# Pooling attention and an MLP mixer in one kernel: rows 0 to 4 of the plan laid out anew, and the end of the fast units reordered

## The chip, the cores and the metric

The kernel runs on one core of one Trainium2 chip. The metric is the time of one execution on the device, in microseconds (us). The profile's names for the engines are PE (matmuls), DVE (vector), ACT (scalar), POOL (GpSimd) and SP (whose queue issues DMAs). POOL's queue issues DMAs too, and an instruction that waits there holds up the loads behind it.

## What is computed

Attention over keys and values that are averaged over 8 neighbouring rows (576 rows become 72), and then an MLP mixer: token mixing with a residual, channel mixing with a residual.

```python
# q, k, v: (8, 8, 576, 64) float32
k_p = k.reshape(B, H, Sp, pool, D).mean(axis=3)          # pool = 8, Sp = 72
v_p = v.reshape(B, H, Sp, pool, D).mean(axis=3)
scores = scale * np.matmul(q, k_p.transpose(0, 1, 3, 2))
scores = scores - np.max(scores, axis=-1, keepdims=True)
attn = np.exp(scores)
attn = attn / (np.sum(attn, axis=-1, keepdims=True) + 1e-09)
x = np.matmul(attn, v_p)                                 # then (8, 576, 512)
h = np.maximum(x.transpose(0, 2, 1) @ w_tok1, 0.0) @ w_tok2   # 576 -> 256 -> 576
u = x + h.transpose(0, 2, 1)
h2 = np.maximum(u @ w_ch1, 0.0) @ w_ch2                  # 512 -> 1536 -> 512
out = u + h2                                             # (8, 576, 512) float32
```

## The kernel before

All matmuls are bf16. The program has a head, in which batch 0 is brought through attention and token mixing, and then nine units. Unit n (0 to 7) does the channel mixing of the first 512 rows of batch n; unit 8 does that of the last 64 rows of all batches together (u_tails). A unit has 45 steps, 0 to 44, each a few matmuls. Between the steps of a unit the work of the batches ahead is issued, by hand: PLAN has a row for each unit, which names for a step what is issued behind it. Each engine runs its own instructions in the order in which they were issued, and engines wait for each other by semaphores, so PLAN is the order of every engine's queue. A name such as 2.K0 is batch 2's operation K0; the Tile framework's manual schedule keeps the order as written.

**The units.** Steps 0 to 23 are the first product (l1_tile): 12 blocks of four matmuls of 512 columns, two steps each (L526), and an ACT relu into GT (L530). Steps 24 to 44 are the second product as seven products of 12 matmuls of 256 columns, three steps each (L680), in the manner of Strassen and Winograd: sums of parts of GT (=1 to =4, one DVE operation of 128x1536 each, L554 and L566, in g_sums) are multiplied by sums of parts of w_ch2 (w0 to w3, L554, made once in unit 0). Each product's bank is evacuated by a DVE addition (L723) into s1, s2, s4, s5 or the output tile o, which SP stores (L545). Units 7 and 8 use a scheme with seven products for the first layer too (l1_fast, L641): 21 products of four matmuls in the order of ORDER, named A to C for three groups and 1 to 7 for the product; some are kept on ACT, others added by DVE (L625) and then put through a relu (L628 on DVE, L654 on ACT).

**Attention of one batch b.** lq, lk, lv: loads, on POOL's queue (L121, L131). K0, K1, V0, V1: the sums over 8 rows for four heads, three POOL operations (L177, L178, then L181 for keys or L183 for values); k0, v0, v1 are the same on DVE; vpool0 and vpool1 do it with matmuls on PE. kpT: the keys transposed on PE (L225) and copied by ACT (L227). Q0, Q1: the queries transposed in blocks on DVE (L287). s0 to s2: scores on PE (L300), exp on ACT (L309). av0 to av4: 128 rows each (av4: the last 64), eight matmuls (L388) into one of two PSUM buffers (ps_two, "p" in the profile, shared with the scores), then on DVE a reciprocal of the denominators (L392) and one multiplication (L331). aw0 to aw4: the same with the multiplication as eight ACT instructions of 64 columns.

**Token mixing.** at0, at1: five matmuls (L400) and an ACT relu (L402). u0 to u4: two matmuls (L422; u4 for two batches together, L417) and a DVE addition of the residual (L423). Then u has to be transposed for the channel mixing. For batches 0 to 2, t0 to t3: PE transposes (L431), copied by ACT (L432). Batches 3 to 7 go by way of DRAM: M0, M2, M4 write u out (L441, on SP), M reads back the parts of M0 and M2 in four DMAs (L453, SP, tile v) and MT that of M4, and T0 to T5 are DVE block transposes of v (L465).

**Gates.** "g" is a memset of one element on DVE (L809) and a copy of it on POOL (L810). POOL's queue, the loads in it among it, goes no further than that copy before DVE has come to the memset; the next memset waits for the copy before it.

**PSUM.** Beside the two buffers of ps_two there are four banks, p1a to p1d, which take and give hand out in the order in which they come free, when the program is recorded.

Of the kernel before, what the change touches and what calls it, by code (L numbers as in the profile page):

```python
# [35 lines left out]
def kernel(  # L36
# [565 lines left out]
    def l1_fast(n, uT):  # L602
# [20 lines left out]
        def add(g, k, ps, row, half):  # L623
            dst = GT[:, half, row * NH + 2 * g:row * NH + 2 * g + 2]
            nc.vector.tensor_tensor(out=dst, in0=ps, in1=kept[g, k], op=ALU.add)  # L625
            if g > 0:
# [1 line left out]
                nc.vector.tensor_scalar(out=dst, in0=dst, scalar1=0.0, scalar2=None, op0=ALU.max)  # L628
# [32 lines left out]
    ORDER = "A1 A2 B1 B2 A6 C1 C2 A5 A7 B6 A3 B5 B7 A4 C6 B3 C5 C7 B4 C3 C4"  # L661

    def unit_fast(n, u):
        last = n == B
# [63 lines left out]
        def store_part(cols, engines):  # L728
            def go(i):
                if len(engines) == 2:  # L730
                    engines[i].dma_start(out=tail_rows(1, cols)[:, i], in_=ob[:, i, cols])
                elif i == 1:
                    engines[0].dma_start(out=tail_rows(1, cols), in_=ob[:, :, cols])
# [4 lines left out]
        x, y = bank(last), bank()  # L738
        s1 = keep("s1")
        yield from product(x, lambda m: GT[:, 0, m], lambda m: w_ch2[:, m, lo], True,  # L740
                           plus(part(s1), part(x), residual(0, 0)), last)
# [142 lines left out]
```

## Time and profile before

| | us |
|---|---|
| median of 3 runs | 264.68 (263.78 to 265.58) |
| the profiled execution | 265.02 |
| its span, first to last instruction | 263.2 |

The granted clock of PE was 0.999 in it. The units stand in the trace like this (by the first matmul of line 526 in each, from PE's timeline): unit 0 from 24.32 us, 1 from 57.40, 2 from 87.46, 3 from 115.53, 4 from 146.26, 5 from 170.54. A row of a timeline gives the start in us, the duration, engine and line, the operation, out and in by the program's names, partitions by elements, the count of like instructions run together, and in brackets the engine's idle time before it with what ended it.

```profile
core 0: us, PE busy (x) PEld busy (x) DVE busy (x) ACT busy (x) POOL busy (x), PEclk, DMA share, GB/s
24.32:57.40 33.08, 31.78 (x271) 20.20 (x274) 25.59 (x46) 15.89 (x26) 18.60 (x22) 1.00 1.22 208
57.40:87.46 30.06, 29.49 (x287) 18.29 (x293) 21.66 (x37) 19.49 (x32) 28.93 (x26) 1.00 0.54 100
87.46:115.53 28.07, 27.70 (x241) 16.55 (x241) 21.01 (x42) 13.06 (x21) 25.38 (x30) 1.00 0.69 144
115.53:146.26 30.73, 29.66 (x255) 17.81 (x255) 24.97 (x51) 13.55 (x23) 26.28 (x23) 1.00 0.75 156
146.26:170.54 24.28, 24.23 (x197) 14.79 (x197) 17.84 (x35) 11.98 (x20) 16.94 (x18) 1.00 0.53 126
```

These are units 0 to 4: length, busy time of each engine with its instructions, the granted clock, the DMA share and rate.

### The profile page before, as it was taken

The page shows a single profiled execution, that of the slowest core. Times are in us where ns is not written, and L with a number is a line of the kernel's source. Part 1 is how long each engine was busy: PE and PEld are TensorE (multiplying, and loading weights), DVE is VectorE, ACT ScalarE, POOL GpSimd, SP SyncE. Part 2 cuts the span into 40 slices and gives each one's busy share as a digit, 9 for nine tenths or more (in the row PEclk, how much of TensorE's full clock was granted, in tenths as well). Part 3 has the DMA queues.
Part 4 walks back from the last instruction along what each step waited for, and adds up shares of the span by engine and source line. Part 5 has one row for each costly group of instructions (what it writes and reads, how often), then busy time and mean ns, then how long its engine had stood idle before and what let it go on. Part 6 is the DMA issues. An engine that isn't in the chain of part 4 may idle for free. (4 is left out here: it accounts for less than half of the span.)

```text
span 263.2 us, 5488 instructions
## 1 busy us (share of the span) xinstructions
PE 254.0 (97%) x2171; PEld 167.7 (64%) x2193; DVE 195.7 (74%) x400; ACT 119.0 (45%) x195; POOL 166.1 (63%) x177
## 2 busy tenths in 40 slices
PE   8999999989999999999998999999999999999994
PEld 2785466754667544774476447754684478888883
DVE  3557469986787665896599686863696389999994
ACT  2355763149537466415640565255625421712700
POOL 8667326899999999978879992798407922100000
PEclk9999999999999999999999999999999999999999
DMA  7999999993079928599645932650315052602404
GB/s 148 187 198 207 205 207 208 206 225 75 4 127 145 163 86 168 133 185 249 127 152 94 215 130 66 97 156 1 126 37 161 2 157 63 181 0 49 114 2 159
DMA packets 31706, 34.31 MB, mean 130 GB/s; under 512 B 3136, under 2 KB 23744, under 8 KB 31680
## 3 DMA queue, kind: packets, MB, share of 16 engines
q0 software_dynamic: 17632, 17.64, 42.4%
q1 hardware_dynamic: 13632, 15.93, 20.4%
q8 instruction: 17, 0.28, 0.5%
q10 hardware_dynamic: 416, 0.39, 0.5%
q14 instruction: 9, 0.07, 0.1%
HBM read 38.99 MB, written 12.58 MB: 196 GB/s over the span
## 5 line engine op out<-in xcount | busy, mean ns | idle before, releaser
L526 PEld LDWEIGHTS <-w_ch 128*128 128x128 bf16 x336 | 30.2, 98 | 33.4 <-issue 2.7
L680 PEld LDWEIGHTS <-area 128*128 128x128 bf16 x432 | 41.4, 98 | 7.5 <-issue 1.0
L810 POOL COPY flag<-flag 1x1 f32<-1x1 f32 x41 | 12.5, 304 | 43.1 <-DVE flag L809 43.0
L309 ACT ACTIVATE ex<-p 72x768 bf16<-72x768 f32 x42 | 31.5, 802 | 17.1 <-PE p L300 17.1
L680 PEld LDWEIGHTS <-GT 128*128 128x128 bf16 x324 | 30.7, 98 | 7.5 <-issue 1.6
L178 POOL TENSOR_TENSOR t<-t 72x512 f32<-72x512 f32 x23 | 32.4, 1409 | 1.8
L526 PE MATMUL p1c<-uT,w_ch 128*128 128x512 bf16 x100 | 28.0, 379 | 0.2
L177 POOL TENSOR_TENSOR t<-kr 72x1024 f32<-72x1024 bf16 x12 | 25.5, 2121 | 0.4
L177 POOL TENSOR_TENSOR t<-vr 72x1024 f32<-72x1024 bf16 x11 | 23.4, 2123 | 2.4 <-DMA vr<-in_v_dram 1.9
L331 DVE TENSOR_TENSOR x<-p,den 128x512 bf16<-128x512 f32 x32 | 22.1, 691 | 1.1
L526 PE MATMUL p1b<-uT,w_ch 128*128 128x512 bf16 x75 | 21.3, 379 | 0.4 <-issue 0.2
L530 ACT ACTIVATE GT<-p1c 128x512 bf16<-128x512 f32 x26 | 15.5, 597 | 12.3 <-PE p1c L526 8.5
L526 PE MATMUL p1a<-uT,w_ch 128*128 128x512 bf16 x72 | 20.5, 379 | 0.3
L526 PE MATMUL p1d<-uT,w_ch 128*128 128x512 bf16 x74 | 19.9, 379 | 0.2 <-issue 0.2
L530 ACT ACTIVATE GT<-p1b 128x512 bf16<-128x512 f32 x20 | 11.9, 596 | 15.3 <-PE p1b L526 8.8
L530 ACT ACTIVATE GT<-p1d 128x512 bf16<-128x512 f32 x19 | 11.4, 599 | 14.0 <-PE p1d L526 8.5
L388 PEld LDWEIGHTS <-ex 72*128 72x128 bf16 x280 | 12.9, 98 | 7.5 <-DVE x L331 2.0
L423 DVE TENSOR_TENSOR u<-p1d,x 128x512 bf16<-128x512 f32 x11 | 8.0, 727 | 11.9 <-PE p1d L422 11.0
L554 DVE TENSOR_TENSOR area<-GT 128x1536 bf16<-128x1536 bf16 x9 | 11.4, 1263 | 6.9 <-ACT AT L402 5.2
L388 PE MATMUL p<-vp,ex 72*128 72x65 bf16 x280 | 14.4, 194 | 1.0 <-DVE x L331 0.5
L121 POOL DMA_DIRECT2D kr<-in_k_dram x17 | 10.9, 646 | 5.4 <-PE p1c L526 2.0
L680 PE MATMUL p1a<-area,area 128*128 128x256 bf16 x108 | 14.3, 273 | 0.0
(235 smaller groups left out, 536.6 us busy)
## 6 DMA issues: line engine op xcount, KB each, us to landing
out_dram<-o SPq DMA_DIRECT2D x32, 256.0 KB, 4.1
qb<-in_q_dram POOLq DMA_DIRECT2D x7, 576.0 KB, 10.3
kr<-in_k_dram POOLq DMA_DIRECT2D x7, 512.0 KB, 8.9
vr<-in_v_dram POOLq DMA_DIRECT2D x7, 512.0 KB, 14.4
w_ch<-in_moe_w_ch_dram POOLq DMA_DIRECT2D x5, 512.0 KB, 14.5
mem<-u SPq DMA_DIRECT2D x10, 256.0 KB, 2.2
v<-mem SPq DMA_DIRECT2D x20, 128.0 KB, 2.9
area<-in_q_dram SPq DMA_DIRECT2D x2, 288.0 KB, 3.0
```

The costliest lines, as they stand in the source:

```text
L121: nc.gpsimd.dma_start(out=t[j0:j1, h0:h1].rearrange("j h i d -> j h (i d)"), in_=src[b, h0:h1].rearrange("h (j i) d -> j h (i d)", i=POOL) ...
L177: eng.tensor_tensor(out=t4[:, 0:n], in0=t[:, hs, 0:4], in1=t[:, hs, 4:8], op=ALU.add)
L178: eng.tensor_tensor(out=t4[:, 0:n, 0:2], in0=t4[:, 0:n, 0:2], in1=t4[:, 0:n, 2:4], op=ALU.add)
L309: nc.scalar.activation(out=dst, in_=src, func=AF.Exp, scale=scale)
L331: nc.vector.tensor_tensor(out=dst, in0=view, in1=den[:, :, :, None].broadcast_to([n, a, 4, D]), op=ALU.mult)
L388: nc.tensor.matmul(out=ps[:, h // 4, (h % 4) * (D + 1):(h % 4 + 1) * (D + 1)], lhsT=st["ex"][:, h * S + n0:h * S + n0 + P], rhs=st["vp"][: ...
L423: nc.vector.tensor_tensor(out=rows_of(c), in0=blocked(ps), in1=blocked(x), op=ALU.add)
L526: nc.tensor.matmul(out=ps, lhsT=w_ch1[:, kk, m * P:(m + 1) * P], rhs=uT[kk], start=(kk == 0), stop=(kk == 3))
L530: nc.scalar.activation(out=GT[:, :, m, :], in_=ps.rearrange("p (h n) -> p h n", h=2), func=AF.Relu)
L554: eng.tensor_tensor(out=out, in0=a, in1=b, op=ALU.subtract)
L680: nc.tensor.matmul(out=ps[i] if split else ps[:, i], lhsT=chunk(u, i, a(m)), rhs=w(m), start=start and m == 0 and (i == 0 or split), stop= ...
L810: nc.gpsimd.tensor_copy(out=flag[:, 1:2], in_=flag[:, 0:1])
```

## The change

HEAD and rows 5 to 8 of PLAN stay. Rows 0 to 4 are written anew: the same operations at other steps, with these differences in kind: 1.av0, 2.av3, 4.av1 and 4.av2 become 1.aw0, 2.aw3, 4.aw1 and 4.aw2 (normalised on ACT); 5.K0 on POOL becomes 5.k0 on DVE; 36 gates instead of 41 in these and the later rows together, at other steps, with the loads of batches 5 to 7 behind other ones; the block transfers of batches 3 to 5 (M, MT, T) at other steps.

```diff
-    {0: "2.lk 0.u1 1.kpT 1.Q0 1.Q1", 3: "0.u0 3.lq 2.lq", 6: "1.s0 0.u2", 8: "g", 9: "0.u3 1.s1", 10: "1.vpool1 2.lv", 12: "1.s2 1.vpool0", 13: "=3", 14: "1.av1 1.av2", 17: "1.av0", 18: "1.av4 g", 19: "w0", 20: "3.lv 1.av3", 22: "w1", 23: "g =1 =2", 24: "3.lk", 25: "=4", 26: "1.at0 g", 27: "2.K0", 28: "w3 1.at1", 30: "g", 31: "1.u2", 32: "2.K1", 33: "1.u0 2.V0", 34: "1.u1", 35: "w2", 37: "1.t2", 40: "1.u3", 41: "1.t0", 42: "1.t3", 43: "1.t1 2.Q0 1.u4", 44: "g 2.kpT 2.Q1 3.Q0"},
-    {1: "2.v1 2.s0", 4: "3.K0", 8: "3.K1 2.s2", 11: "g", 12: "2.s1", 15: "3.Q1", 16: "2.av3", 17: "4.lq 2.av1", 18: "4.lk", 19: "2.av0", 20: "2.av4", 23: "2.av2 =1 g", 25: "2.at0 =2", 26: "g", 27: "3.kpT", 28: "2.at1 =4", 31: "2.u3", 32: "3.s2 4.Q1", 33: "2.u2", 34: "5.lk", 35: "3.s0", 36: "3.V1 =3", 37: "2.t3", 39: "3.s1 3.V0 4.lv g 2.u0", 41: "2.u1 2.t2", 42: "2.t0 g", 43: "2.t1 3.av0", 44: "3.av4"},
-    {2: "3.av2", 4: "4.K1", 6: "4.K0 3.av1", 7: "3.av3", 11: "3.at1", 12: "g", 13: "3.at0", 15: "=3", 17: "4.Q0 3.u1 4.kpT", 18: "6.lk 3.u3 4.V1 3.u0", 20: "3.u2 4.s2", 21: "3.u4 3.M0", 23: "4.V0 g", 24: "3.M2", 25: "=1", 26: "5.lq 4.s0", 27: "=2", 28: "g", 29: "=4 6.lq", 30: "4.s1 3.M", 32: "3.T3", 33: "5.lv 3.T0", 35: "g", 36: "4.av1 g", 37: "3.M4 3.T2 3.T1", 38: "6.lv", 40: "g", 41: "3.MT", 43: "4.av2", 44: "4.av4"},
-    {3: "5.K1 4.av0", 5: "4.av3 5.K0", 7: "6.Q0", 8: "4.at1", 10: "4.at0 g", 11: "5.Q1", 12: "5.Q0", 13: "3.T4", 15: "3.T5 5.kpT 4.u3 4.u2 4.u1", 16: "5.V1 g", 17: "5.s0", 18: "=3", 20: "4.u0", 24: "5.s1", 25: "=1 4.M0 4.M2", 26: "=2 =4", 28: "5.V0 5.s2 g", 30: "g", 32: "5.av0 7.lq", 35: "5.av2", 36: "5.av1 4.M", 40: "5.av4 5.av3", 41: "4.T0", 42: "4.T1 4.T3", 43: "4.T2 5.at0 5.at1"},
-    {2: "7.Q0 5.u3 6.K1", 6: "7.lk", 7: "5.u0", 8: "5.u2", 10: "5.u1 6.K0", 11: "6.kpT", 12: "6.V1", 14: "5.M0", 17: "6.V0 5.M2", 18: "6.s0", 20: "=3 7.Q1", 22: "6.Q1", 23: "5.M =1", 24: "6.s1 g", 26: "g", 28: "=2", 29: "5.T1 5.T0", 31: "g", 33: "6.s2", 34: "=4 g", 36: "7.lv", 38: "g", 41: "6.av3", 42: "5.T3", 43: "5.T2", 44: "5.u4 6.av0"},
+    {0: "0.u0 2.lk 0.u1 1.Q0 1.Q1", 2: "1.kpT", 3: "3.lq 2.lq", 5: "0.u3", 6: "1.s0", 7: "0.u2", 8: "2.lv", 9: "1.s1", 11: "1.vpool1", 12: "1.s2 1.vpool0", 13: "=3 g", 14: "1.av2", 15: "1.av1", 17: "1.aw0", 18: "1.av4 g", 19: "w0", 20: "3.lv 1.av3", 22: "w1", 23: "g =1 =2 3.lk", 25: "1.at1 1.at0 =4", 26: "g 2.K1", 27: "2.K0", 28: "w3", 29: "2.V0", 33: "1.u0", 34: "1.u1", 35: "1.u2", 36: "w2", 37: "2.Q1 1.t2", 40: "1.u3", 41: "1.t0", 42: "1.t3", 43: "g 1.t1 3.Q0 2.Q0 1.u4"},
+    {0: "2.kpT", 1: "2.v1", 3: "2.s0", 8: "3.K1 2.s2", 9: "3.K0", 11: "4.lq", 12: "2.s1", 15: "3.Q1", 16: "2.aw3", 17: "2.av1", 18: "g", 20: "2.av0", 21: "2.av4", 23: "2.av2 =1", 24: "4.lk", 25: "g", 26: "3.kpT 2.at1", 27: "=2", 28: "2.at0 =4 g", 31: "2.u3 4.Q1", 32: "3.s2", 33: "2.t3 2.u2", 35: "3.s0 3.V1", 36: "=3", 37: "3.V0", 38: "g 2.u1", 39: "4.lv 3.s1 2.u0", 40: "5.lk", 41: "4.Q0 2.t2 2.t0", 43: "2.t1 3.av0 3.av2"},
+    {4: "4.K1", 6: "3.av3 3.av4", 9: "3.av1 4.K0", 12: "g 3.at1", 13: "6.lk", 14: "=3 3.at0", 18: "4.kpT 4.V1", 19: "3.u1 4.V0", 20: "3.u0 3.u3", 21: "3.u2 3.u4", 23: "4.s2", 24: "3.M0 3.M2", 25: "=1", 26: "3.M4", 27: "=2", 28: "4.s0", 29: "=4", 30: "3.M", 31: "4.s1 3.MT 3.T3 3.T0", 32: "g 5.lq 5.lv", 34: "3.T1", 35: "4.av4 4.aw1", 36: "3.T2", 38: "g 6.lq", 40: "g", 42: "4.aw2 6.lv"},
+    {1: "4.av0", 3: "5.K1", 5: "4.av3", 8: "4.at1", 9: "4.at0 5.k0", 10: "5.Q0", 11: "4.u2", 12: "5.V0", 13: "4.u1", 15: "5.kpT 4.u3 5.V1", 16: "4.M2", 17: "5.s0", 18: "=3 5.Q1", 19: "6.Q0", 22: "4.u0", 23: "5.s1", 24: "4.M0", 25: "3.T4 =1 3.T5", 26: "=2", 27: "=4", 28: "g", 29: "4.M", 30: "5.s2", 32: "5.av0", 35: "5.av2", 37: "5.av1", 40: "5.av3 5.av4", 42: "4.T3 4.T1 4.T0", 43: "4.T2 5.at0 5.at1"},
+    {2: "6.K1", 5: "7.lq 7.lk 5.u3", 6: "5.u2", 8: "5.u0", 10: "6.K0", 11: "6.kpT", 12: "5.u1 6.V1 6.V0", 13: "5.M0", 16: "6.s0", 17: "5.M2", 18: "5.M", 20: "7.Q1", 21: "7.Q0", 22: "6.Q1 g", 23: "=1", 24: "6.s1 =3", 26: "g", 28: "=2", 29: "6.s2 5.T1", 30: "g", 32: "g 7.lv 5.T3", 34: "5.T0 =4", 36: "g", 37: "g", 41: "5.T2", 42: "6.av3", 44: "6.av0 5.u4"},
```

In the fast first layer (units 7 and 8) product C7's relu goes to ACT, the banks of groups B and C are given back after the fourth product of each group, and the first product of the second layer (12 matmuls, in three parts, X) is put around C4. In unit 8 the evacuation of the second product (y) is moved behind that of the third (s5). g_sums can make halves of a sum ("a", "b"), which no row of PLAN asks for. The last product of unit 8 is written out as a loop, with the same matmuls and stores.

```diff
-                nc.vector.tensor_scalar(out=dst, in0=dst, scalar1=0.0, scalar2=None, op0=ALU.max)
+                if g > 1 and k == 5:
+                    nc.scalar.activation(out=dst, in_=dst, func=AF.Relu)
+                else:
+                    nc.vector.tensor_scalar(out=dst, in0=dst, scalar1=0.0, scalar2=None, op0=ALU.max)
...
-                if g == NM // 4 - 1:
-                    for i in range(4):
-                        give(bank[1 + i % 2, i // 2])
+                if g > 0:
+                    give(bank[g, 1])
+                    give(bank[g, 0])
...
-    ORDER = "A1 A2 B1 B2 A6 C1 C2 A5 A7 B6 A3 B5 B7 A4 C6 B3 C5 C7 B4 C3 C4"
+    ORDER = "A1 A2 B1 B2 A6 C1 C2 A5 A7 B6 A3 B5 B7 A4 C6 B3 C5 C7 B4 C3 X C4 X X"
...
+        s1, first = keep("s1"), None
+        uT = [u["uT"][:, kk, :] for kk in range(4)]
+        if n in FAST:
+            step = l1_fast(n, uT)
+            for t in ORDER.split():
+                if t != "X":
+                    step("ABC".index(t[0]), int(t[1]))
+                    yield
+                    continue
+                if first is None:
+                    x = bank(last)
+                    first = product(x, *first_args(x))
+                next(first)
+                yield
...
-        yield from product(z, lambda m: SG[:, 0, m], lambda m: TW[:, 0, m], True,
-                           plus(part(s5), part(z), residual(1, 1)))
+
+        def fifth(e):
+            plus(part(s5), part(z), residual(1, 1))(e)
+            if last:
+                first_cols(e)
+                give(y)
+
+        yield from product(z, lambda m: SG[:, 0, m], lambda m: TW[:, 0, m], True, fifth)
```

More of the change, by code (lines that the diff above doesn't have):

```diff
@@ L726, in plus, with store_part @@
             return go
-        def store_part(cols, engines):
+        def store_part(cols):
             def go(i):
[L730 to L733, printed above, removed]
-            return go
+                if i == 1:
+                    nc.scalar.dma_start(out=tail_rows(1, cols), in_=ob[:, :, cols])
+            return go
@@ new lines, in first_args @@
+        def first_args(x):
+            return (lambda m: GT[:, 0, m], lambda m: w_ch2[:, m, lo], True, plus(part(s1), part(x), residual(0, 0)), last)
+        s1, first = keep("s1"), None
[12 more added lines that the diff above has]
+                yield
+            for _ in range(3):
+                yield
+        else:
+            for m in range(NM):
+                yield from l1_tile(n, m, uT)
@@ L736, in unit_fast @@
         SG, TW = sums_tile("S", "area"), sums_tile("T", "area2")
         oa, ob = (outp.tile([P, 2, DM], FP32, name="o") for _ in range(2))
[L738 to L741, printed above, removed]
+        if first is None:
+            x = bank(last)
+            yield from product(x, *first_args(x))
+        y = bank()
+        first_cols = plus(cols_of(oa, 0), part(y), part(s1))
@@ L760, in unit_fast @@
             yield from product(x, lambda m: SG[:, 2, m], lambda m: TW[:, 2, m], False,
-                               plus(cols_of(ob, 1), part(x), part(s5), store_part(hi, [nc.scalar])), True)
-            yield from product(x, lambda m: GT[:, 1, NH + m], lambda m: TW[:, 3, m], False,
-                               plus(cols_of(ob, 0), part(x), residual(1, 0), store_part(lo, [nc.scalar, nc.sync])), True)
+                               plus(cols_of(ob, 1), part(x), part(s5), store_part(hi)), True)
+            r = residual(1, 0)
+            for i in range(2):
+                for ks in (slice(0, 2),):
+                    cols = slice(ks.start * P, ks.stop * P)
+                    for m in range(NH):
+                        nc.tensor.matmul(out=x[i][:, cols], lhsT=chunk(u, i, GT[:, 1, NH + m]), rhs=TW[:, 3, m, cols],
+                                         start=False, stop=(m == NH - 1), skip_group_check=True)
+                    view = [v.rearrange("p (k a f) -> p k a f", a=4, f=D // 2) for v in (ob[:, i, cols], x[i][:, cols])]
+                    nc.vector.tensor_tensor(out=view[0], in0=view[1], in1=r(i)[:, ks], op=ALU.add)
+                (nc.sync if i else nc.scalar).dma_start(out=tail_rows(1, lo)[:, i], in_=ob[:, i, lo])
+                yield
         else:
```

24 lines of the change are left out of this document (8 added, 16 removed).

## Prediction

> **What bounds the kernel now.** First the head of the page, then the list of what PE waits for.
>
> ```profile
> span 263.2 us, 5488 instructions
> PE 254.0 (97%) x2171; PEld 167.7 (64%) x2193; DVE 195.7 (74%) x400; ACT 119.0 (45%) x195; POOL 166.1 (63%) x177
> ```
>
> PE is busy for 97% of the span; no other engine passes 74%. The change has the same matmuls as before, so it can win only what PE stands idle, and lose only by new stands. These are the waits behind the head:
>
> ```profile
> PE p1c L225 <- POOL kp L181: 1.1, 1, 1.1
> PE p L388 <- DVE x L331: 0.5, 1, 0.5
> PE p L388 <- POOL vp L183: 0.4, 2, 0.2
> PE p1b L400 <- DVE x L331: 0.2, 1, 0.2
> ```
>
> (columns: total us, times, longest). They sum to 2.2, but the list counts from the modelled end of a matmul, which lies behind the moment at which the next could start. So I reread them from starts in PE's timeline:
>
> ```profile
> 56.02 0.23 PE L225 MATMUL p1c<-ident,kp 72*128 72x72 bf16 x2
> 57.33 0.24 PE L225 MATMUL p1c<-ident,kp 72*128 72x72 bf16 x2 [1.08 <-POOL kp L181]
> 57.40 0.81 PE L526 MATMUL p1a<-uT,w_ch 128*128 128x512 bf16 x2
> ...
> 138.27 0.60 PE L680 MATMUL p1d<-area,GT 128*128 128x256 bf16 x4
> 139.39 0.43 PE L388 MATMUL p<-vp,ex 72*128 72x65 bf16 x8 [0.52 <-DVE x L331]
> ...
> 230.30 0.60 PE L641 MATMUL p1d<-uT,vr 128*128 128x256 bf16 x4
> 231.03 0.60 PE L641 MATMUL p1c<-qb,w_ch 128*128 128x256 bf16 x4
> ...
> 248.95 0.60 PE L641 MATMUL p1b<-uT_tails,vr 128*128 128x256 bf16 x4
> 249.67 0.60 PE L641 MATMUL p1a<-qb,w_ch 128*128 128x256 bf16 x4
> 250.11 1.47 PE L680 MATMUL p<-w_ch,GT 128*128 128x256 bf16 x12
> ...
> 254.04 1.47 PE L680 MATMUL p<-area,area 128*128 128x256 bf16 x12
> 255.58 1.47 PE L680 MATMUL p1a<-w_ch,area 128*128 128x256 bf16 x12
> ```
>
> Two transposes take 0.07 from start to start (57.33 to 57.40), so the second pair of batch 2's kpT could have begun at 56.09 and lost 1.24. Four matmuls of 256 columns take 0.44 (249.67 to 250.11). The four at 138.27 were done with their turn at 138.71, the av behind them came at 139.39: 0.68, which is 0.16 more than the 0.52 of the list. With the same 0.16 added, the two vp waits are 2 x 0.36 = 0.72 and at0's is 0.36. Units 0 to 4 thus hold 1.24 + 0.68 + 0.72 + 0.36 = 3.0, and I estimate another 0.5 in stands too short for the list, about three of that same 0.16. At the end, 230.30 to 231.03 and 248.95 to 249.67 are 0.73 and 0.72 for four: 0.29 and 0.28 lost. From 254.04 twelve matmuls need 3 x 0.44 = 1.32, the next came after 1.54: 0.22. So the most that can be had is 3.5 + 0.8 = 4.3, 1.6% of the time. All the rest of the new plan counts only through what it costs.
>
> **The change part by part.**
>
> *Batch 2's keys (unit 0), gain 1.24.* POOL sums K0, then K1, and kpT wants both. Now K1 and K0 are issued at steps 26 and 27, V0 behind them, and kpT goes one step back, from the last step of unit 0 (44) to step 0 of unit 1.
>
> ```profile
> 47.59 2.12 POOL L177 TENSOR_TENSOR t<-kr 72x1024 f32<-72x1024 bf16 x1
> 49.79 1.27 POOL L178 TENSOR_TENSOR t<-t 72x512 f32<-72x512 f32 x1
> 51.14 1.67 POOL L181 TENSOR_TENSOR kp<-t 72x256 bf16<-72x256 f32 x1
> ...
> 51.17 0.94 DVE L554 TENSOR_TENSOR area<-w_ch 128x1536 bf16<-128x1536 bf16 x1
> ```
>
> From 47.59, one half takes 2.12 + 1.27 + 0.84 with its gaps of 0.1, about 4.45 (the 1.67 has a wait in it, 0.94 less 0.1 of DVE's w2). Two halves and one such wait of 0.86 end at 47.59 + 2 x 4.45 + 0.4 = 56.9, since only part of that 0.86 falls in; PE is at kpT at 57.1. The wait goes, with 0.2 to spare. What is late next is w2.
>
> *w2 against POOL.* w2 moves one step on, and K0's first operation begins about 47.59 + 4.2 = 51.8, w2 about 51.5. Such pairs exclude each other:
>
> ```profile
> 153.65 2.12 POOL L177 TENSOR_TENSOR t<-vr 72x1024 f32<-72x1024 bf16 x1
> ...
> 154.06 2.53 DVE L554 TENSOR_TENSOR area<-GT 128x1536 bf16<-128x1536 bf16 x1 [0.39 <-ACT GT L530]
> ```
>
> DVE's operation, 0.94 alone, began 0.41 behind POOL's and ended at 156.59, 0.82 behind POOL's end at 155.77. Whoever is first holds the other. By my times DVE is first by 0.3 and POOL pays: nothing on PE. The other way DVE is held for 2.1 and PE, which has 0.5 of evacuations in hand, for 1.6. I take 0 and keep 1.6. The Trainium skill, "SBUF — State Buffer", section "Who interferes with whom", has the same rule: a DVE instruction with two SBUF inputs and a GpSimd instruction that reads SBUF lock each other out for a whole instruction, and issue order decides; this trace agrees (2.53 against 0.94). It speaks against 5.k0 below too, and is a rival.
>
> *Four normalisations on ACT, cost 0.8.* An av leaves DVE a reciprocal and one multiplication; aw gives ACT eight multiplications of 64 columns.
>
> ```profile
> 39.37 0.21 DVE L392 RECIPROCAL den<-p 64x8 f32<-64x8 f32 x1
> 39.62 0.69 DVE L331 TENSOR_TENSOR xt<-p,den 64x512 bf16<-64x512 f32 x1
> ...
> L402 ACT ACTIVATE AT<-p1d 128x512 bf16<-128x512 f32 x5 | 3.0, 597 | 4.4 <-PE p1d L400 4.0 <-PE p1c L526 0.4
> L374 ACT ACTIVATE AT<-p1d 128x256 bf16<-128x256 f32 x1 | 0.4, 383 | 1.1 <-PE p1d L366 1.1
> ```
>
> (the last two: count, busy, mean ns). 256 columns fewer save 214 ns, 0.84 ns each, so 64 columns cost 597 - 448 x 0.84 = 222 ns, eight 1.8 us; bounds 1.2 (back to back) and 8 x 0.383 = 3.1. That holds one of the two PSUM buffers about twice as long as 0.21 + 0.69. In unit 0 the next-but-one av (av3, step 20) therefore waits for av4's buffer, which lay with DVE: av4's eight matmuls 0.43 (as at 139.39), then 0.21 + 0.69 and two hand-overs between engines of some 0.05, 1.4 in all, against 1.1 of cover: an estimated 0.25 for the turn of the eight and two steps of two 512-column matmuls, 0.43 each by the 256-column time: 0.3. Next, 1.u2 now stands between u1 and t2, t2's transposes wait for its DVE addition (0.72, less what u3 covers): 0.5 more. So 0.8, with 0.3 and 1.3 as ends. 2.aw3, 4.aw1 and 4.aw2 have two steps or more to the next use of their buffer: 0.
>
> *Gates.* 36 instead of 41. A gate is a DVE memset that POOL's copy waits for; POOL's pooling and loads behind it are held till DVE is there. Loads 5.lq, 5.lv (step 32 of unit 2), 7.lq and others are issued later, but their users follow over ten steps behind: 0.
>
> *Units 1, 3, 4.* Unit 1: V0's POOL operation meets =3; DVE held partly: 0.2 (0 to 0.6). Unit 4: 0.05; there a gate now stands ahead of =3. Unit 3: K0 of batch 5 goes to DVE. What it costs is shown by v1 of batch 2:
>
> ```profile
> 58.87 1.69 DVE L177 TENSOR_TENSOR t<-vr 72x1024 f32<-72x1024 bf16 x1
> 60.59 1.64 DVE L178 TENSOR_TENSOR t<-t 72x512 f32<-72x512 f32 x1
> 62.27 0.84 DVE L183 TENSOR_TENSOR vp<-t 72x256 bf16<-72x256 f32 x1
> ```
>
> 4.2 us of DVE behind at0, in the first product, when DVE evacuates nothing and next PE needs u2's and u1's adds (steps 11, 13): about 0.3 (0 to 0.7). POOL gets 4.4 back, so V0 and V1 of 5 are early and the vp waits go (0.72, above). At 139.39 the cause was DVE's at unit 3's end, now lighter as =2, =4 meet no POOL work.
>
> *Batch 3's block transposes (unit 2), cost 0.3.* T3 and T0 now both follow M and MT at step 31; DVE stands in T3 until the blocks are back from DRAM, with evacuations and aw1's reciprocal behind it.
>
> ```profile
> 106.87 1.80 SPq L453 DMA_DIRECT2D v<-mem  x4
> ...
> DMA to landing us min/median/max: 2.4/2.9/7.9
> ...
> 111.33 0.77 DVE L465 STREAM_TRANSPOSE uT<-v 128x256 uint32<-128x256 uint32 x2
> ```
>
> (the middle line is tile v between 105 and 112.) The four reads are out by 108.3 and land 2.9 later, 111.2; T3 ran at 111.33 with no idle. M0 and M2 are now sent together; the reads can go between 105.3 and 106.9, so land between 109.6 and 111.2. By its step, DVE is at T3 near 109, and PE has till about 109.5: 0.1 to 1.7, and I take 0.3, since M0 and M2 go early.
>
> *The tail, gain 0.7.* Second-layer matmuls are put before and behind C4: four of them, 0.44, cover the 0.29 and the 0.28. C7's relu (0.29 on DVE, below) goes to ACT.
>
> ```profile
> 249.65 0.29 DVE L628 TENSOR_SCALAR GT<-GT 128x512 bf16<-128x512 bf16 x1
> ...
> 253.31 0.68 DVE L723 TENSOR_TENSOR o<-p1c,s 128x512 f32<-128x512 f32 x1
> ...
> 254.78 0.74 DVE L723 TENSOR_TENSOR s<-p1a,u_tails 128x256 f32<-128x256 f32 x2
> ```
>
> 254.78 + 0.74 = 255.52 is what 255.58 waited for; moving the 0.68 of 253.31 behind it frees the bank before 255.36. Of 0.8 I count 0.1 back, as =3 and s2 now come closer to their product (0 to 0.3).
>
> *Sum.* Gains 3.5 + 0.7 = 4.2; costs 0.8 + 0.2 + 0.3 + 0.3 + 0.05 = 1.65; net 2.55. The profiled execution took 265.02 (span 263.2 and 1.8 around it): 262.5. It lies 0.34 over the median of the runs, 264.68, so 262.1 beside that.
>
> **Rivals.** *All stalls go.* None of my 1.65 shows: 264.68 - 4.2 = 260.5. For it: each new stand is a matter of a few tenths. Against: PSUM has two buffers for av, and ACT's 1.8 is certain.
>
> *DVE locked out by POOL.* w2 behind K0's first operation costs 1.6, and =1 behind V1 in unit 3 another 0.7 (2.53 against 0.94, less what PE has in hand): 262.1 + 1.6 = 263.7 for the first, 264.4 for both. It decides if POOL's K0 starts before w2: 0.3 between them.
>
> *Slower: DVE held at T3.* The later reads of the same batch, MT, came back so:
>
> ```profile
> DMA to landing us min/median/max: 7.9/9.0/9.3
> ...
> 123.28 0.77 DVE L465 STREAM_TRANSPOSE uT_tails<-v 128x256 uint32<-128x256 uint32 x2 [0.18 <-DMA v<-mem]
> ```
>
> (tile v from 111.5 on.) With 9.0 instead of 2.9 the blocks land 6.1 later, about 115.7 by the early reads and 116.7 for a middle one; DVE stands, its evacuations with it, and PE loses what lies behind 109.5: 6 to 7. That gives 262.1 - 0.3 + 6.2 = 268 to 269. It is slower by over 1% (267.33) once the landing passes 115.0. Against it: MT's reads ran beside the loads of batches 5 and 6, which are now behind the gate that follows T3; only 6.lk may be in flight.
>
> **How the numbers follow.** My sum 0.50, all gone 0.22, locked out 0.20, held at T3 0.08. One per cent, about what can be told from no change here, is 262.03 and 267.33. My sum lies on the first bound, so its 0.50 goes half to each side: faster 0.25 + 0.22 = 0.47, same 0.25 + 0.20 = 0.45, slower 0.08. The range goes from 260.3 (all gone, and the last 0.1 of the stands with it) to 264.6 (both locks, 264.4, with unit 2's costs at 0.5): T3's case lies outside.
>
> **What would show it.** In the profile after: kpT with no POOL wait, near 57; a wait for DVE at av3 of batch 1 of about 0.3; w2 of 0.94; T3 with under a microsecond of idle for "DMA v<-mem"; no 0.7 spacing ahead of C4; four ACT rows of eight small multiplications at about 222 ns. Wrong if w2 or =1 shows 2 us or more, if T3 waits for microseconds, or if PE's list of waits has a new line of over a microsecond in a place that I gave 0.

## The result

| | median us | runs |
|---|---|---|
| the kernel before | 264.09 | 7 (263.78 to 265.83) |
| the changed kernel | 262.90 | 7 (262.57 to 263.40) |

The ratio is 0.9938, with a 95% interval of 0.9910 to 0.9965: 0.6% faster, 1.6 us (0.9 to 2.4), which is within 1%. It is the ratio of the means (262.92 and 264.57); the medians alone would give 1.2 us. Taken again later beside 26 runs of the kernel before, it was 0.9925 (0.9904 to 0.9946), 262.67 against 264.60 by median. The forecast was 262.1 with a range of 260.3 to 264.6. Here and in the experiments the ratio with its interval decides; it can differ from the quotient of the two medians, in the experiments by up to 0.0012. Two runs are left out of the ratios, one of 269.86 us of the kernel before and one of 1478.49 us of the variant with the gate, 1.av0 and y's evacuation together.

The head of the page after, and what PE waits for in it:

```profile
span 260.8 us, 5503 instructions
PE 253.0 (97%) x2172; PEld 167.8 (64%) x2193; DVE 194.9 (75%) x391; ACT 125.4 (48%) x229; POOL 159.0 (61%) x168
```

```profile
PE p1a L807 <- DVE area L868: 1.2, 1, 1.2
PE p1d L235 <- DMA kr<-in_k_dram: 0.5, 1, 0.5
PE p L345 <- ACT ex L325: 0.4, 1, 0.4
PE p1b L422 <- DVE flag L840: 0.3, 1, 0.3
PE p L674 <- DVE s L717: 0.2, 1, 0.2
PE p1d L431 <- DVE u L423: 0.2, 1, 0.2
PE p L388 <- DVE xt L331: 0.2, 1, 0.2
```

The first three lie in the head. Of the four lines of before none is left; four new ones of 0.2 to 0.3 stand in their place. A stand is time that PE loses between two matmuls. It is measured as in the prediction, from start to start, against the spacing that matmuls keep elsewhere (0.216 us for 512 columns, 0.109 for 256, 0.032 for 65). PE's stands by unit, good to about 0.1, are these:

| unit | before | changed | the old rows again, with the new end |
|---|---|---|---|
| 0 | 1.43 | 0.89 | 1.33 |
| 1 | 0.44 | 0.41 | 0.46 |
| 2 | 0.63 | 0.28 | 0.62 |
| 3 | 1.55 | 0.16 | 0.69 |
| 4 to 6 | 0.11 | 0.22 | 0.11 |
| 7 and 8 | 0.94 | 0.70 | 0.72 |
| sum | 5.10 | 2.66 | 3.93 |

5.10 - 2.66 = 2.44 is the 2.4 by which the spans differ. The length from the first matmul of unit 0 to the first one of the last product says the same without any spacing: 233.92 before, 231.44 changed, 232.70 in the last column. The head ahead of it took between 23.7 and 24.8 us in the fourteen profiles of this document, though HEAD is the same in all of them; so small differences between spans say little by themselves.

The two profiled executions, 265.02 and 262.58, are 2.44 apart, the means of the runs 1.65: the one of before lay 0.45 above its mean, the changed one 0.34 below. The last column shows one place where executions differ: the old rows stand 0.69 in unit 3 in another one, not 1.55.

In unit 0 the prediction's small terms can be read one by one. These are rows of ACT, DVE, POOL and PE of the changed kernel in it:

```profile
38.59 1.75 ACT L335 ACTIVATE x<-p,den 128x64 bf16<-128x64 f32 x8
```

```profile
39.28 0.69 DVE L331 TENSOR_TENSOR xt<-p,den 64x512 bf16<-64x512 f32 x1
...
50.86 0.71 DVE L423 TENSOR_TENSOR u<-p1d,x 128x512 bf16<-128x512 f32 x1
51.48 0.98 DVE L554 TENSOR_TENSOR area<-w_ch 128x1536 bf16<-128x1536 bf16 x1
```

```profile
50.80 0.84 POOL L181 TENSOR_TENSOR kp<-t 72x256 bf16<-72x256 f32 x1
51.72 2.73 POOL L177 TENSOR_TENSOR t<-kr 72x1024 f32<-72x1024 bf16 x1
```

```profile
40.04 0.43 PE L388 MATMUL p<-vp,ex 72*128 72x65 bf16 x8 [0.17 <-DVE xt L331]
...
51.63 0.40 PE L431 MATMUL p1d<-ident,u 128*128 128x128 bf16 x4 [0.18 <-DVE u L423]
```

The eight multiplications take 1.75 together (1.8 was expected); av3 at 40.04 waits for av4's normalisation, which ended at 39.97, and t2 for u2's addition (51.57). w2 at 51.48 is 0.24 ahead of POOL's K0 (0.3 was expected), keeps its 0.98, and POOL pays with 2.73 instead of 2.12.

The end of the changed kernel, DVE and then PE:

```profile
251.63 0.75 DVE L717 TENSOR_TENSOR s<-p1d,u_tails 128x256 f32<-128x256 f32 x2
252.30 0.68 DVE L717 TENSOR_TENSOR o<-p1b,s 128x512 f32<-128x512 f32 x1
252.90 0.95 DVE L554 TENSOR_TENSOR area<-GT 128x1536 bf16<-128x1536 bf16 x1
253.76 0.75 DVE L717 TENSOR_TENSOR s<-p,u_tails 128x256 f32<-128x256 f32 x2
```

```profile
252.52 1.47 PE L674 MATMUL p1d<-w_ch,area 128*128 128x256 bf16 x12
254.23 1.47 PE L674 MATMUL p<-area,area 128*128 128x256 bf16 x12 [0.24 <-DVE s L717]
255.69 1.47 PE L789 MATMUL p<-area,GT 128*128 128x256 bf16 x12
```

s5 now comes before y's evacuation, and its product starts on time at 252.52. But DVE has no gap in these rows, and what was put behind s5 now stands ahead of s2 (253.76): the next product starts 1.71 later instead of 1.31, and the last 1.46 later: 0.40 + 0.15 lost again.

### The profile page after: what moved, and what is told of

Its sections match the earlier page's. It is cut to its first block, busy times and chain, and to the rows that moved or that the text cites. A ratio compares the mean times of both kernels' runs of the same rounds, so it can differ in the third digit from the quotient of the medians.

```text
span 260.8 us, 5503 instructions
## 1 busy us (share of the span) xinstructions
PE 253.0 (97%) x2172; PEld 167.8 (64%) x2193; DVE 194.9 (75%) x391; ACT 125.4 (48%) x229; POOL 159.0 (61%) x168
## 4 chain that ended last, share of the span: by engine, by line
PE 89%; DVE 5%; DMA 2%; issue 2%; ACT 0%; POOL 0%; DVEq 0%; ACTq 0%; POOLq 0%
PE p1a L674 8%; PE p1c L526 8%; PE p1d L674 7%; PE p1a L526 7%; PE p1b L674 7%; PE p1b L526 7%; PE p1d L526 6%; PE p1c L674 5%; PE p L388 4%; PE p L300 3%; PE p L647 2%; DMA kr<-in_k_dram 2%; PE p1d L400 2%; PE p1b L400 2%; PE p1c L422 2%
## 5 line engine op out<-in xcount | busy, mean ns | idle before, releaser
L841 POOL COPY flag<-flag 1x1 f32<-1x1 f32 x35 | 10.2, 292 | 48.5 <-DVE flag L840 48.4
L178 POOL TENSOR_TENSOR t<-t 72x512 f32<-72x512 f32 x22 | 30.6, 1389 | 1.7
L526 PE MATMUL p1c<-uT,w_ch 128*128 128x512 bf16 x89 | 24.6, 379 | 0.2
L177 POOL TENSOR_TENSOR t<-kr 72x1024 f32<-72x1024 bf16 x11 | 23.9, 2177 | 0.4
L526 PE MATMUL p1a<-uT,w_ch 128*128 128x512 bf16 x82 | 22.3, 380 | 0.2
L526 PE MATMUL p1d<-uT,w_ch 128*128 128x512 bf16 x76 | 21.6, 379 | 0.2
L331 DVE TENSOR_TENSOR x<-p,den 128x512 bf16<-128x512 f32 x28 | 19.4, 691 | 1.0
L530 ACT ACTIVATE GT<-p1a 128x512 bf16<-128x512 f32 x21 | 12.6, 602 | 14.8 <-PE p1a L526 7.4
L530 ACT ACTIVATE GT<-p1c 128x512 bf16<-128x512 f32 x23 | 13.9, 604 | 8.3 <-PE p1c L526 8.3
L423 DVE TENSOR_TENSOR u<-p1c,x 128x512 bf16<-128x512 f32 x11 | 8.0, 729 | 7.9 <-PE p1c L422 6.0
## 6 DMA issues: line engine op xcount, KB each, us to landing
w_ch<-in_moe_w_ch_dram POOLq DMA_DIRECT2D x5, 512.0 KB, 14.7
```

Source lines behind the costliest of these rows:

```text
L177: eng.tensor_tensor(out=t4[:, 0:n], in0=t[:, hs, 0:4], in1=t[:, hs, 4:8], op=ALU.add)
L178: eng.tensor_tensor(out=t4[:, 0:n, 0:2], in0=t4[:, 0:n, 0:2], in1=t4[:, 0:n, 2:4], op=ALU.add)
L331: nc.vector.tensor_tensor(out=dst, in0=view, in1=den[:, :, :, None].broadcast_to([n, a, 4, D]), op=ALU.mult)
L526: nc.tensor.matmul(out=ps, lhsT=w_ch1[:, kk, m * P:(m + 1) * P], rhs=uT[kk], start=(kk == 0), stop=(kk == 3))
L530: nc.scalar.activation(out=GT[:, :, m, :], in_=ps.rearrange("p (h n) -> p h n", h=2), func=AF.Relu)
L841: nc.gpsimd.tensor_copy(out=flag[:, 1:2], in_=flag[:, 0:1])
```

## The experiments

Each was timed beside the kernel before. The first four, the next four and the last four make three groups; each group shares its runs of the kernel before.

**The rows alone.** Rows 0 to 4 of the new PLAN in the old code.

> Rows 0 to 4 of the new plan with the old end of units 7 and 8. Theory: the gain is made in units 0 to 4, by about 2.3 us of PE's stands, so this is 2.0 to 2.4 us faster than the kernel before in the profile, and PE's timeline shows again the 0.73 for four matmuls ahead of C4 in units 7 and 8. Rival (the prediction's own split): 1.85 from the plan, 0.7 from the end, so this is 1.9 faster at most. Second rival: the profile of before was an unlucky draw, and the plan is worth under 1 us.

Measured: 264.15 against 264.84, ratio 0.9986 (0.9965 to 1.0007). PE's stands sum to 3.7: units 0 to 2 are as long as in the changed kernel (32.44, 30.13 and 27.72 us against 32.43, 30.14 and 27.72), units 7 and 8 stand as before (0.94), and unit 3 has 0.97 instead of 0.16. PE's row of that stand, and DVE's rows ahead of it:

```profile
125.89 0.29 PE L225 MATMUL p1d<-ident,kp 72*128 72x72 bf16 x4 [0.62 <-DVE u L423]
```

```profile
122.30 2.23 DVE L181 TENSOR_TENSOR kp<-t 72x256 bf16<-72x256 f32 x1
...
125.15 0.68 DVE L423 TENSOR_TENSOR u<-p1d,x 128x512 bf16<-128x512 f32 x1
```

kpT of batch 5 waits there, not for the keys, which were done at 124.53, but for its bank p1d: the addition of u2 that empties it stands behind k0 and 5.Q0 on DVE and ended at 125.83. The stand is 0.79, and it is not in the trace of the changed kernel, though the rows are the same. From the last product to the end of the span it took 5.6 us instead of the 5.0 of before: the last two stores landed 2.6 after their issue, in before 2.3 and 2.0. So the span is only 0.7 shorter. The theory's 2.0 to 2.4 fell, and so did the prediction's split; the second rival, under 1 us, is what came.

**The end alone.** The old PLAN in the new code.

> The old plan with the new end of units 7 and 8. Prediction: 0.7 us faster (0.27%). Theory from the trace after: only about 0.3, because DVE runs without a gap through unit 8 and the wait comes back ahead of the product behind s2; PE's timeline shows 1.7 instead of 1.31 for the product before it.

Measured: 264.25 against 264.84, 0.9989 (0.9965 to 1.0012). Units 7 and 8 stand 0.72 instead of 0.94: 0.2, as the theory had it, not 0.7; the time alone could not tell the two apart. And unit 3 of the same old rows stood 0.69 here. POOL's first operation of batch 5's V and DVE's =1, in the first profile of before and then in this one, with what they waited for in brackets:

```profile
125.96 2.12 POOL L177 TENSOR_TENSOR t<-vr 72x1024 f32<-72x1024 bf16 x1 [1.89 <-DMA vr<-in_v_dram]
131.90 1.95 DVE L566 TENSOR_TENSOR area<-GT 128x1536 bf16<-128x1536 bf16 x1 [1.25 <-ACT GT L530]
```

```profile
125.47 2.12 POOL L177 TENSOR_TENSOR t<-vr 72x1024 f32<-72x1024 bf16 x1 [1.10 <-DMA vr<-in_v_dram]
132.28 1.08 DVE L569 TENSOR_TENSOR area<-GT 128x1536 bf16<-128x1536 bf16 x1 [1.25 <-ACT GT L530]
```

Unit 3 began at 115.53 in before and at 115.92 here, so POOL began this operation 0.88 later in before; the load that it waits for had landed 14.7 us after its issue there, 13.8 here. POOL's next V operation began at 130.91 in before, 0.99 ahead of =1, and at 130.43 here, 1.85 ahead: it was nearly over. That lateness is the stand of 0.36 at 136.44 (POOL's, for vp) and 0.52 of the 0.68 at 139.39 (DVE's, behind =1).

The halves alone give 0.14% and 0.11%, the whole change 0.6% to 0.75%. The intervals don't exclude that the halves add up, but it isn't shown that they do. In the profile of the rows alone unit 3 is 0.84 longer than in the changed kernel, and the end, from the last product on, 0.46; whether its other runs lost as much isn't shown either.

**y's evacuation last.**

```diff
             plus(part(s5), part(z), residual(1, 1))(e)
-            if last:
-                first_cols(e)
-                give(y)
...
-        s2 = keep("s1")
+        s2 = keep("s4" if last else "s1")
...
+            def third(i):
+                plus(cols_of(ob, 1), part(x), part(s5), store_part(hi))(i)
+                if i == 1:
+                    first_cols(slice(0, 2))
+                    give(y)
+                    store(n, 0, oa)
...
```

> The changed kernel with y's evacuation put behind both halves of the seventh product's in unit 8, so that s2 comes 0.6 us earlier. Theory (DVE's order is what holds PE): the 0.41 ahead of the product that waits for s2 and the 0.15 ahead of the last one go, 0.5 us less than the changed kernel. Rival (DVE is simply full there): the wait goes to the last product or to the last additions, and 0.15 or less is left.

Measured: 263.29 against 264.84, 0.9950 (0.9935 to 0.9966). PE's stands in units 7 and 8 are gone (0.00), but the span did not gain: the last product started at 255.85 and the span ended at 262.0, 6.1 later; in the changed kernel it is 255.69 and 260.8, 5.1. The store of the first half left SP at 257.1 instead of 255.3, just ahead of the last ones. The stand had moved into the stores. The theory's 0.5 did not come. Of the rival, that 0.15 or less is left holds, but the time went neither to the last product nor to the last additions, which ended 1.9 us after that product's start in both kernels.

**That, with 1.av0 and another order of u0 to u2.** `1.aw0` becomes `1.av0`; `33: "1.u0", 34: "1.u1", 35: "1.u2"` becomes `33: "1.u2", 34: "1.u1", 35: "1.u0"`.

> As the run before, with 1.aw0 back on DVE and batch 1's u2 issued ahead of u0. Theory: av3's wait of 0.33 and t2's of 0.46 in unit 0 go too, 1.3 us less than the changed kernel in all, 261.6 by its median of 262.9. Rival: w0 and the gate behind it hold DVE instead, and av3 waits for the multiplication as long as before, so only t2's 0.46 and the end's 0.5 show.

Measured: 263.91 against 264.84, 0.9974 (0.9954 to 0.9993). av3's stand is gone, t2's 0.34 is not (the bank that it writes is that of the last u, whichever that is), and a new one of 0.37 has come, at the transposes two steps on. Its cause is w2; POOL, DVE and PE:

```profile
51.02 0.84 POOL L181 TENSOR_TENSOR kp<-t 72x256 bf16<-72x256 f32 x1
51.08 1.60 DVE L554 TENSOR_TENSOR area<-w_ch 128x1536 bf16<-128x1536 bf16 x1
53.99 0.38 PE L431 MATMUL p1c<-ident,u 128*128 128x128 bf16 x4 [0.20 <-DVE s L717]
```

POOL's last operation of K1 had begun 0.06 ahead of w2. This is the rival of the prediction in which DVE is locked out by POOL, with a shorter operation: w2 lost 0.6, and PE 0.37 instead of 1.6.

**The changed kernel again.**

> The changed kernel once more, beside the kernel before and the next three. In its first profile the read-back of batch 3's blocks was issued at 104.3 us, POOL's 5.K1 ran from 115.2, and 5.k0 on DVE took 1.21 + 1.21 + 0.42; in three variants with the same rows around it the read-back was issued at 105.3, 5.K1 ran from 116.3, 5.k0 took 2.0 + 1.2 + 2.2 and kpT of batch 5 waited 0.4 to 0.6. Theory: the spills' landing varies by a microsecond between executions, and this run shows either of the two, not a mixture; 263.0 to 264.0 by median. Rival: the variants' other edits made the shift, and this run has 5.k0 at 2.84 again.

Measured: 262.67 against 264.60, 0.9925 (0.9904 to 0.9946). 5.K1 from 114.9, k0 1.31 + 1.21 + 2.23, kpT without a wait: a mixture, which the expectation had excluded, and a median below its 263.0 to 264.0.

**The gate ahead of T3.** `31: "4.s1 3.MT 3.T3 3.T0", 32: "g 5.lq 5.lv"` becomes `31: "4.s1 3.MT g 3.T3 3.T0", 32: "5.lq 5.lv"`.

> One edit in the changed kernel: the gate of 5.lq and 5.lv is put ahead of T3 and T0 instead of behind them. Theory (T3 waits for DRAM, and the gate behind it passes that on to POOL's queue, so that 5.K1 comes late and meets 5.k0): 5.K1 starts by 115.3 whatever the read-back does, 5.k0 takes under 3.5 us in all and kpT of batch 5 waits for nothing. Rival: the loads, issued earlier, meet the read-back, T3 waits for 2 us or more and PE stands for 1 us or more at T3.

Measured: 263.40 against 264.60, 0.9961 (0.9943 to 0.9980). T3 waited 1.18, and 5.K1 still began at 116.3, not by 115.3: DVE, late behind T3, is late at the gates of steps 38 and 40 as well (memsets at 113.95 and 114.32, in the changed kernel at 112.79 and 113.16). kpT stood 0.49. So the lateness does pass on through gates, but not through that one alone, and the theory's numbers fell; the rival's 2 us at T3 and 1 us on PE did not come either.

**5.K0 back on POOL.** `9: "4.at0 5.k0"` becomes `9: "4.at0 5.K0"`.

> The changed kernel with 5.K0 back on POOL. Prediction: putting it on DVE gives POOL 4.4 us back and takes the 0.36 for vp in unit 3 away. So here kpT of batch 5 waits for POOL (K1 from 115.2 to 116.3, two halves of 4.4, kpT due at 125.1: 0 to 0.6) and the vp wait of unit 3 is back, 0.4 to 1.0 slower than the changed kernel. Rival: since 5.k0 meets POOL's operations anyway, POOL alone is as fast, and nothing is lost.

Measured: 263.86 against 264.60, 0.9963 (0.9945 to 0.9980). Units 3 and 4 stand 0.25 + 0.50 = 0.75, against 0.40 in the changed kernel; in the variants in which kpT waits it is 0.9 to 1.2. kpT waited for nothing and no wait for vp came back; a stand of 0.33 at the start of unit 4's first product did. So in these profiles DVE's k0 is worth about 0.35 when it misses POOL, and in the five in which kpT stands it is worse than POOL's K0 by 0.2 to 0.5.

**The gate, 1.av0 and y's evacuation last, together.**

> The changed kernel with the gate ahead of T3, 1.aw0 back on DVE and y's evacuation behind the seventh product's in unit 8. Theory: av3's 0.33, the end's 0.56 and unit 3's 0.56 go, so this is 0.9 less than the changed kernel when that is at its best and 1.4 less when it is not. Rival: each stand moves on to the next use of DVE, and the gain over the changed kernel is under 0.4.

Measured: 263.65 against 264.60, 0.9968 (0.9948 to 0.9988). av3's stand is gone and w2 took 1.60 again, with the order of u0 to u2 as in the changed kernel: giving DVE back the one multiplication of 0.69 is enough to put w2 (51.15) behind POOL's operation. Unit 0 took 32.43 us, exactly as in the changed kernel. The rival holds: the stands moved on.

**Batch 2's keys alone, in the kernel before.** K1 and K0 at steps 26 and 27, kpT at step 0 of unit 1.

```diff
-    26: "1.at0 g", 27: "2.K0",
-    32: "2.K1", 33: "1.u0 2.V0",
-    44: "g 2.kpT 2.Q1 3.Q0"},
-    {1: "2.v1 2.s0",
+    26: "1.at0 g 2.K1", 27: "2.K0",
+    33: "1.u0 2.V0",
+    44: "g 2.Q1 3.Q0"},
+    {0: "2.kpT", 1: "2.v1 2.s0",
```

> The kernel before with the one move of batch 2's keys: K1 and K0 together at steps 26 and 27 of unit 0 and kpT at step 0 of unit 1. Prediction: POOL is done at 56.9 and the 1.24 goes. Theory from the trace after: POOL is done only some 0.3 earlier than in before, about 57.0, and PE comes to kpT 0.43 later in its order; so 0.4 to 0.6 of the wait stays, and in the changed kernel it went because PE had already stood 0.8 at av3 and t2. 264.0 against 264.6.

Measured: 264.08 against 264.25, 0.9993 (0.9970 to 1.0016). POOL and PE in it:

```profile
56.42 0.84 POOL L181 TENSOR_TENSOR kp<-t 72x256 bf16<-72x256 f32 x1
...
57.31 0.30 PE L225 MATMUL p1a<-ident,kp 72*128 72x72 bf16 x4 [0.63 <-POOL kp L181]
```

POOL is done at 57.26, as in before (57.27), and PE still stands 0.57. In the changed kernel POOL was done at 56.72 and PE came with 0.8 of other stands behind it. The theory holds for the wait; the time shows nothing.

**s2 first, then y, and the seventh product between the halves.** In the changed kernel:

```diff
-            if last:
-                first_cols(e)
-                give(y)
...
-        s2 = keep("s1")
+        s2 = keep("s4" if last else "s1")
+
+        def second(e):
+            plus(part(s2), part(x), residual(0, 1))(e)
+            if last and e == 1:
+                first_cols(slice(0, 2))
+                give(y)
...
+            def third(i):
+                plus(cols_of(ob, 1), part(x), part(s5), store_part(hi))(i)
+                if i == 0:
+                    second_cols(slice(0, 2))
+                    give(z)
+                    store(n, 0, oa)
```

second_cols is the evacuation of z that stood behind its own product.

> The changed kernel with s2 ahead of y's evacuation and the seventh product's evacuation between the halves of the next, in unit 8; the store of the first half goes out 0.4 later than in the changed kernel, 1.4 earlier than in the run in which y's evacuation came last. Theory: the 0.40 and 0.15 on PE go and the stores stay in their time, 0.3 to 0.5 off the span from the last waits on. Rival (the end is set by DVE's work and the stores, not by PE): the last store is issued no more than 0.15 earlier, and the span does not change.

Measured: 263.64 against 264.25, 0.9970 (0.9947 to 0.9993). SP's rows of this kernel, then of the changed one, each with the landing times of tile o at the end:

```profile
257.09 0.37 SPq L804 DMA_DIRECT2D out_dram<-o  x1
...
DMA to landing us min/median/max: 2.7/3.1/3.3
```

```profile
257.65 0.37 SPq L793 DMA_DIRECT2D out_dram<-o  x1
...
DMA to landing us min/median/max: 2.0/2.5/2.8
```

PE's last product in this kernel:

```profile
254.85 1.75 PE L800 MATMUL p<-area,GT 128*128 128x256 bf16 x12
```

The 0.40 and 0.15 are gone, but PE now stands 0.28 inside the last product: its row takes 1.75, the others 1.47. From the last product's start (254.85) to the end of the span (260.9) it takes 6.05, where the changed kernel took 5.1. The last four stores now leave within 1.7 us instead of 2.3, and the last three of them take 0.5, 1.0 and 0.7 longer (the landing line gives minimum, median and maximum, issue to landing). Counted from unit 0 on, the last store leaves 0.24 earlier and the span is 0.42 longer. The rival holds in the main, the span isn't shorter: what is won on PE is lost in the last product and at the stores.

**M4's write behind the read-back.** `26: "3.M4"` goes behind `3.M` at step 30.

> The changed kernel with M4's write behind the read-back M on SP instead of ahead of it. Theory (M4's 256 KB share the DMA engines with M0 and M2, whose landing starts the read-back): the read-back is issued by 104.3 in every execution, T3 waits 0.4 or less, POOL's 5.K1 starts by 115.2 and kpT of batch 5 waits for nothing; 262.7 by median. Rival: the landing varies for another reason, and the read-back still comes at 105.3 or later.

Measured: 262.70 against 264.25, 0.9941 (0.9916 to 0.9966). Here the read-back left at 104.29, T3 waited 0.76 (0.4 or less was expected), 5.K1 began at 115.3, and kpT did not wait. But the next run speaks against the theory.

**Both.**

> Both edits of the two runs before together. Theory: the gains add, 0.3 to 0.5 under m4_late. Rival: the end gives nothing, and this is within 0.2 of m4_late.

Measured: 263.16 against 264.25, 0.9957 (0.9937 to 0.9977). The same edit, and the read-back left at 105.29, T3 waited 1.28, 5.K1 began at 116.2. So M4 isn't what holds M0 and M2 up; that theory fell, and what makes the write of u land at 104.3 or 105.3 stays open. The edit of the end gave nothing on top, as the rival had it, but 263.16 is 0.46 above the 262.70 of M4's edit alone, not within 0.2. None of the variants is faster than the changed kernel.

## What varies: one place in unit 3

All ten executions with the new row 3 and 5.k0 on DVE, from the DVE, POOL and SP timelines:

| kernel | read-back leaves | 5.K1 begins | k0's three operations | kpT stands |
|---|---|---|---|---|
| changed | 104.3 | 115.2 | 1.21 1.21 0.42 | 0 |
| changed, again | 103.9 | 114.9 | 1.31 1.21 2.23 | 0 |
| M4 late | 104.3 | 115.3 | 1.50 1.22 0.42 | 0 |
| s2 first | 105.3 | 116.3 | 1.21 1.64 0.95 | 0 |
| both | 105.3 | 116.2 | 2.02 1.21 0.42 | 0 |
| y last | 105.3 | 116.2 | 1.98 1.22 2.23 | 0.56 |
| rows alone | 105.6 | 116.5 | 2.21 1.21 2.23 | 0.79 |
| gate first | 105.5 | 116.3 | 1.91 1.22 2.23 | 0.49 |
| gate, av0, y | 105.7 | 116.4 | 1.98 1.22 2.23 | 0.56 |
| av0, u order, y | 105.3 | 116.3 | 1.95 1.21 2.23 | 0.52 |

The read-back leaves 0.05 us behind the landing of M2's write each time. That write landed 2.1 to 2.5 us after its issue in the first three, 3.0 to 3.5 in the others; counted from unit 0 on, the read-back leaves at 80.0 to 80.4 and at 81.0 to 81.4, so the head isn't the reason.

DVE of the changed kernel and of the run with y last, the first near one end of the table and the second near the other:

```profile
118.71 1.21 DVE L177 TENSOR_TENSOR t<-kr 72x1024 f32<-72x1024 bf16 x1
119.95 1.21 DVE L178 TENSOR_TENSOR t<-t 72x512 f32<-72x512 f32 x1
121.20 0.42 DVE L181 TENSOR_TENSOR kp<-t 72x256 bf16<-72x256 f32 x1
```

```profile
118.79 1.98 DVE L177 TENSOR_TENSOR t<-kr 72x1024 f32<-72x1024 bf16 x1
120.81 1.22 DVE L178 TENSOR_TENSOR t<-t 72x512 f32<-72x512 f32 x1
122.06 2.23 DVE L181 TENSOR_TENSOR kp<-t 72x256 bf16<-72x256 f32 x1
```

and POOL in the same two:

```profile
117.38 1.26 POOL L178 TENSOR_TENSOR t<-t 72x512 f32<-72x512 f32 x1
118.72 1.90 POOL L181 TENSOR_TENSOR kp<-t 72x256 bf16<-72x256 f32 x1
121.31 2.29 POOL L177 TENSOR_TENSOR t<-vr 72x1024 f32<-72x1024 bf16 x1 [0.70 <-DMA vr<-in_v_dram]
```

```profile
118.43 1.26 POOL L178 TENSOR_TENSOR t<-t 72x512 f32<-72x512 f32 x1
119.77 1.70 POOL L181 TENSOR_TENSOR kp<-t 72x256 bf16<-72x256 f32 x1
121.60 2.40 POOL L177 TENSOR_TENSOR t<-vr 72x1024 f32<-72x1024 bf16 x1
```

In the first pair DVE is in by 0.01 at 118.71, POOL's 118.72 waits for it; the last operation of k0 (121.20) is 0.11 ahead of POOL's 121.31. In the second pair POOL is first both times (118.43, and 121.60 against 122.06), and DVE pays 0.77 and 1.81. kpT stands when k0 takes over 5 us from 118.8 on. At T3 itself the lateness costs PE nothing; this is T3 of the run with y last:

```profile
109.78 0.77 DVE L465 STREAM_TRANSPOSE uT<-v 128x256 uint32<-128x256 uint32 x2 [1.29 <-DMA v<-mem]
```

In the ten executions DVE stands idle 0.31 to 1.68 us ahead of T3, and unit 2 is 27.72 us long in all of them. So a lateness of 1 us in DRAM can come out as half a us on PE some 20 us later. It need not: with s2 first and with both edits the read-back was late and kpT did not wait, since DVE was first at 118.39 in the one, and POOL's next V operation came only at 122.55 in the other.

The five executions without a stand there (two of the changed kernel) belong to ratios of 0.9925 to 0.9970, 0.9946 in the mean; the five with one have 0.9950 to 0.9986, 0.9968. The difference, 0.6 us, fits the stand, but these kernels differ in other places too, and there is one profile for each, so it isn't shown that their other runs stood likewise.

## Why the prediction was right, and where it was not

**Bound.** PE at 97%, gain and loss through its stands: right, down to the profiles' 2.44 against 2.4. (The rows alone and the edits of the end add that time is also lost behind the last matmul.) The forecast for the profile was 2.55 less; it was 2.4. But "the most that can be had is 3.5 + 0.8 = 4.3" took one execution's stands for those of all. In unit 3 the old rows stood 1.55 in that one, 0.69 and 0.63 in two others (the end alone, batch 2's keys alone). Some 0.9 of what was to be gained hangs on when the load of batch 5's V lands. 2.44 less that 0.9 is about the 1.6 us of the ratio; this is the largest error that the traces show, but how often the runs stood so isn't shown.

**The agreement of the sum is partly luck.** By place, the prediction's gains less costs are 0.44 in unit 0, 0.16 in unit 1, 0.2 in unit 2 (where its 0.5 of short stands lie in before: 0.12, 0.17 and 0.26 at 88.88, 91.05 and 92.01), 1.10 in unit 3, -0.05 in unit 4 and 0.7 at the end. Found are 0.54, 0.03, 0.35, 1.39, -0.11 (units 4 to 6) and 0.24. What the end lacked, units 2 and 3 gave. The number 262.1 also stands on the median of three runs, 264.68; over all seven it is 264.09, and 2.55 less is 261.5, which is 1.4 below the measured median. And the range, up to 264.6, holds the kernel before as well, so that to lie in it says little.

**Batch 2's keys, gain 1.24.** The wait went, but not as "POOL is done at 56.9", "PE is at kpT at 57.1", with "0.2 to spare" has it. Alone, the same move leaves 0.57 of it: POOL was done at 57.26 and PE could have been there at 56.74, earlier than the 57.1, for which the prediction shows no working. The rest went because PE arrives later by the new stands before it. The term was counted in full beside the 0.8 that paid for part of it; unit 0's net, 1.43 - 0.89 = 0.54, agrees with 1.24 - 0.8 all the same.

**aw, cost 0.8.** The stands are 0.33 at av3 and 0.12 + 0.34 ahead of t2, 0.79 in all, and the eight multiplications took 1.75 for 1.8. With 1.aw0 undone, the 0.33 goes and w2 loses its lead instead.

**w2.** Order and lead were right in the changed kernel (0.24 for 0.3); the rival is real, since a shift of the kind of one multiplication brings it about, but its price was 0.35, not 1.6: it met an operation of 0.84, not that of 2.12. The lock did make =3 take over 2 us in the changed kernel, 2.16 in unit 1 and 2.38 in unit 3.

**Unit 1.** 0.2 was expected from =3 meeting V0, and the stand is 0.21, at the bank that =3's lateness holds back. **Unit 2.** 0.3 was expected at T3 and nothing is found there, even with T3 waiting 1.7; the unit's one new stand, about 0.2 inside batch 4's scores at 107.4 to 108.1, comes ahead of T3's start at 108.72 and is there however long T3 waits. So DVE's stand at T3 has more cover than I gave it; the rival's 6 us were never put to the test. What the account lacked is the way out by the gates. **Unit 3.** 0.3 (0 to 0.7) was expected for k0; 0 to 0.79 is found, through u2's addition as forecast, though it is kpT that waits for the bank, and k0 takes from 2.84 to 5.65 us of DVE instead of a fixed 4.2. That "POOL gets 4.4 back" and so the vp waits go was not the reason: with 5.K0 back on POOL they did not return, and one of the two lay at 86.51 in unit 1, before batch 5's keys are summed at all.

**The tail, gain 0.7.** This failed. C4's 0.29 and 0.28 went and s5's 0.22 went; but the 0.1 (0 to 0.3) that the prediction counts back was 0.55, at s2 and the last product, because DVE has no gap from 246 to 255.2 and y's evacuation had only changed places. The net was 0.2. And taking the 0.55 away does not shorten the span: the last stores then leave closer together and land later.

**The forecast's shares.** The result lies between "my sum" and "locked out", on the side of no change by 1%: 0.45 was given to it, 0.47 to faster.

## What to carry to other kernels

Read the stands of a tuned kernel from more than one execution before they are summed: a wait that hangs on a load's landing, or on which of two engines is first by 0.1 us, is there one time and gone the next, and a plan made against one profile can count on only the waits that are in all of them. Take the head off before spans are compared. Where a wait ends because another came before it, try the move alone; it shows how much of the gain is its own. On an engine without a gap, putting one operation behind another only picks who waits; and at the very end the stores count as well as the matmuls.
